# A planner that treats GpSimd and VectorE's two-port SBUF work as holders of one lock

## The chip, the cores and the metric

The kernel runs on one core of a Trainium2 chip. The metric is the device time of one execution in microseconds (us); the number used is the median of several runs. Times of single instructions are in nanoseconds (ns) or us as the profiler recorded them.

The engines are called as in the profile: PE (TensorE matmul), PEld (its weight load), DVE (VectorE), ACT (ScalarE), POOL (GpSimd) and SP (SyncE, which here issues every DMA).

## The reference

The reference is blockwise causal attention followed by two feed-forward layers, all in float32:

```python
scores = scale * np.matmul(q, k.transpose(0, 1, 3, 2))      # q, k, v: 4 x 8 x 576 x 64
scores = np.where(mask, scores, -1e9)                       # block of 64 sees itself and earlier blocks
attn = softmax(scores);  x = (attn @ v) as 2304 x 512
g = x @ w_gate;  x = (g * sigmoid(g) * (x @ w_val)) @ w_out # d_ff 1536
h = x @ w_in;  g = where(h > 0, h, exp(min(h, 0)) - 1)      # d_ff 2048
return g @ w_out
```

## The kernel before

Tokens are handled in 9 chunks of 256. Chunk 0 holds the first block of 64 tokens of every batch; chunks 1 to 8 hold the rest of a batch's tokens, two chunks for each batch. The program has three stages. The first, here called the attention stage, ends at about 470 us; it does the attention and, interleaved with it, the gate and value matmuls of the first layer (PE lines L164 to L166, tile gv). The second multiplies by the first layer's w_out (tile y). The third is the second layer, done with a seven-product scheme (tiles h and o).

Float32 matmuls are made of three products of a high part and a low part: hi x hi, hi x lo, lo x hi. The high part is a cast on ACT, the low part a subtraction. Which engine subtracts matters for this change:

- **Weights.** A conversion unit (`conv_unit`, 24 of them for gate and value, i below 2*K1) loads raw words, makes c on ACT (L142), runs three DVE steps on it (`cv_b`, L150, L152 and L154, all from SBUF to SBUF; the last two read two SBUF tensors), casts the high part wh on ACT (L157) and subtracts the low part wl on POOL (L161).
- **Heads.** For each of 64 heads, POOL makes the low parts of k (`ks`, L409), q (`ql`, L415) and v (`vs`, L422). The first 8 heads skip this. PE multiplies q by k into slo and shi in PSUM; DVE masks, takes the row maximum and scales it (nm, L481); ACT takes the exponential (L491); DVE forms 1/sum in two small steps (sm, L495 and L497). The rows are scaled on ACT for the first 20 heads and on DVE after that (`norm`, L503). PE transposes (L533, L534), ACT casts the high part th, DVE subtracts the low part tl out of PSUM (L542; tt, L568, for the last 64 keys), and PE multiplies by v (tile pv, L548 to L551 and L574). DVE adds the two halves of the result (xf, L589) and subtracts the low part xl of the chunk, from SBUF to SBUF (L596).

The order of the work on each engine is not written by hand. Class `Plan` holds a list of tasks, each with an engine, a cost in ns, a priority and its dependencies. `order` simulates them: again and again it takes the engine that can start soonest, picks among that engine's tasks that can start by then the one of least priority number, and books the engine for the task's cost. The simulated start times give the order in which the instructions are issued; each engine's instructions then run on the chip in that order, each waiting on semaphores for its inputs. In `order` before the change, engines meet only in dependencies; POOL and DVE can both be busy at the same simulated time at no extra cost. Tiles rotate over few buffers (raw 2, c 4, ks 3, ql 3, vs 4, tr 2, gv 2), and the planner also keeps the order in which such buffers are taken.

Of the kernel before, what the change touches and what calls it, by code (L numbers as in the profile page):

```python
# [13 lines left out]
ALU = mybir.AluOpType  # L14
# [27 lines left out]
class Plan:  # L42
# [9 lines left out]
        n = self.count[tag] = self.count.get(tag, -1) + 1  # L52
        return n

    def add(self, eng, ns, fn, prio, reads=(), writes=(), after=(), data=0.0, behind=None):
        i, deps, order = len(self.tasks), set(), set()
        for d in self.groups[behind] if behind else ():
            (order if self.tasks[d][0] == "SP" else deps).add(d)
        self.groups.setdefault(self.group, []).append(i)
        for k in list(reads) + list(writes):  # L60
            tag, n = b = k[:2]
            if tag in self.bufs:
                deps.update(self.users.get((tag, n - self.bufs[tag]), ()))
                order.update(self.users.get((tag, n - 1), ())[:1])
            self.users.setdefault(b, []).append(i)
        for k in list(reads) + list(after):
            if k in self.wr:
                deps.add(self.wr[k])
        for k in reads:
            self.rd.setdefault(k, []).append(i)  # L70
        for k in writes:
            if k in self.wr:
                deps.add(self.wr[k])
            deps.update(self.rd.get(k, ()))
            self.wr[k], self.rd[k] = i, []
        deps.discard(i)
        self.tasks.append((eng, ns, fn, prio, deps, data, order - deps - {i}))

    def order(self):
        T = self.tasks  # L80
        succ, left, est = [[] for _ in T], [len(t[4]) + len(t[6]) for t in T], [0.0] * len(T)
        for i, t in enumerate(T):
            for d in t[4]:
                succ[d].append((i, True))
            for d in t[6]:
                succ[d].append((i, False))
        engines = sorted({t[0] for t in T})
        ready = {e: [i for i, t in enumerate(T) if t[0] == e and not left[i]] for e in engines}
        free, dma, start = dict.fromkeys(engines, 0.0), 0.0, [0.0] * len(T)
        for _ in T:  # L90
            t, e = min((max(free[e], min(est[i] for i in ready[e])), e) for e in engines if ready[e])
            i = min((i for i in ready[e] if est[i] <= t), key=lambda i: (T[i][3], i))
            ready[e].remove(i)
            start[i] = t
            free[e] = end = t + T[i][1] * (2 if e == "PE" and t < WARM else 1)
            if T[i][5] > 0:
                dma = end = max(dma, t + DMA_IN) + T[i][5]
                end += DMA_OUT
            for j, wait in succ[i]:
                lat = 0.0 if e == "NONE" else SELF * (e == "DVE") if T[j][0] == e else LAT  # L100
                est[j] = max(est[j], end + lat + max(0.0, -T[i][5]) * (T[j][0] == "SP") if wait else t + 1.0)
                left[j] -= 1
                if not left[j]:
                    ready[T[j][0]].append(j)
        self.span = max(free.values())
        self.start = start
        return [T[i][2] for i in sorted(range(len(T)), key=lambda i: (start[i], i))]
# [3 lines left out]
def attention_moe_moe_kernel(ctx: ExitStack, tc: tile.TileContext,  # L111
# [116 lines left out]
    def conv_unit(i, prio, after=(), whole=False):  # L228
        r, c, w = ("raw", i, 0), ("c", i, 0), ("w", i, 0)
        add("SP", 450, lambda: cv_dma(i), prio, writes=[r], data=1456)  # L230
        add("ACT", 520, lambda: cv_a(i), prio, [r], [c])
        for p, ns in enumerate((335, 602, 602) if i < 2 * K1 else (500, 700, 750)):
            add("DVE", ns, lambda p=p: cv_b(i, p), prio, [r, c], [c], data=-1000 if p == 2 and i >= 2 * K1 else 0.0)
        if whole:
            return
        add("ACT", 520, lambda: cv_hi(i), prio, [c], [w], after)
        add("POOL", 1330 if i < 2 * K1 else 1500, lambda: cv_lo(i), prio, [c, w], [w])
# [45 lines left out]
    def t0_attn(s, q):  # L283
# [65 lines left out]
        add("DVE", 335, ssum, PT0, [P], [sm])  # L349
        add("DVE", 70, lambda: rec(0), PT0, [sm], [sm])  # L350
        add("DVE", 90, lambda: rec(1), PT0, [sm], [sm])
        add("DVE", 335, lambda: dve.tensor_tensor(st["P"], st["P"], st["sm"].to_broadcast([128, 4, 64]), ALU.mult), PT0, [P, sm], [P])
        add("PE", 218, tr, PT0, [P, ("id", 0, 0)], [tr_k])
        add("ACT", 264, cp, PT0, [tr_k], [pt])
        add("PE", 850, pv, PT0, [pt] + blk("vz"), [pv_k])
# [35 lines left out]
    def a_head(n, prio):  # L391
# [118 lines left out]
            add("DVE", 69, lambda u=u: sc_nm(u), prio, [nk], [nk])  # L510
            add("ACT", .833 * e + 240, lambda u=u: ex(u), prio, [sk, nk], [pk[u], sk2])
        sk2 = [("sm", n, 0), ("sm", n, 1)]
        add("DVE", 70, lambda: rec(0), prio, sk2, sk2)
        add("DVE", 81, lambda: rec(1), prio, sk2, sk2)
        for u, e in ((0, e0), (1, e1)):
            if n < NACT:
                add("ACT", .833 * e + 145, lambda u=u: norm(u), prio, [pk[u]] + sk2, [pk[u]])
            else:
                add("DVE", .521 * e + 129, lambda u=u: norm(u), prio, [pk[u]] + sk2, [pk[u]])

        ch, k = 1 + n // H, h // 2
        xr = slice(64 * j, 64 * j + 64)
# [87 lines left out]
        add("DVE", 335, xf, prio, [pvk, K["xb"]], [("xf", i, j)])  # L610
        if j == 1:
            add("ACT", 307, xh, prio, [("xf", i, 0), ("xf", i, 1)], [("x", ch, ("h", k))])
            add("POOL" if XLP else "DVE", 790 if XLP else 335, xl, prio, [("xf", i, 0), ("xf", i, 1), ("x", ch, ("h", k))], [("x", ch, ("l", k))])


    a_stage = {}
# [495 lines left out]
```

## Time and profile before

| what | value |
|---|---|
| median of 3 runs | 1046.24 us (1044.62 to 1046.64) |
| span of the profiled execution, first to last instruction | 1045.0 us |
| PE busy over the span | 1023.0 us (98%) |
| DVE, ACT, POOL busy over the span | 825.7, 606.3, 286.5 us |
| granted TensorE clock, mean | 0.998 |

The device time of the profiled execution itself is not listed beside its span; the runs lie from 0.4 us below the span to 1.6 us above it. A busy share of 98% for PE does not say that PE is at its peak, since a matmul is recorded as busy until its modelled end, and the next one may already be running: PE's pace is read from its count of matmuls and its waits, stretch by stretch.

### The profile page before, as it was taken

How to read it: one execution, taken by the hardware profiler on the slowest of the kernel's cores; microseconds unless marked ns; L12 is line 12 of the kernel's file. 1: busy time of each engine (PE TensorE's matmuls, PEld its weight loads, DVE VectorE, ACT ScalarE, POOL GpSimd, SP SyncE). 2: the span in 40 equal slices, each digit the busy share in tenths (PEclk: the TensorE clock that was granted, in tenths of full speed). 3: DMA queues.
4: the chain of work that ended last, by engine and by line, in shares of the span. 5: the costliest groups of instructions: out<-in, count | busy, mean ns of one | idle time of the engine just before them, and what ended most of it. 6: DMA issues, size and time to landing. Idle time of an engine off the chain costs nothing.

```text
span 1045.0 us, 19569 instructions
## 1 busy us (share of the span) xinstructions
PE 1023.0 (98%) x6520; PEld 935.1 (89%) x6520; DVE 825.7 (79%) x1967; ACT 606.3 (58%) x1531; POOL 286.5 (27%) x288
## 2 busy tenths in 40 slices
PE   9999899999999999999999999999999999999998
PEld 8678899999999999999977888898888998898897
DVE  6889999988888888877666775889998666876665
ACT  3898787776776677654354555555563443543343
POOL 1267543443444344303233222223210000000000
PEclk9999999999999999999999999999999999999999
DMA  7577557422542254004779988777646433454331
GB/s 177 163 217 207 154 160 202 122 80 87 139 123 81 85 140 122 25 28 134 227 258 321 316 292 282 252 237 235 218 149 211 126 121 121 122 172 121 112 111 61
DMA packets 119366, 170.00 MB, mean 163 GB/s; under 512 B 15840, under 2 KB 75744, under 8 KB 119264
## 3 DMA queue, kind: packets, MB, share of 16 engines
q1 hardware_dynamic: 119264, 168.74, 53.3%
q8 instruction: 52, 0.85, 0.3%
q14 instruction: 50, 0.41, 0.1%
HBM read 130.42 MB, written 38.27 MB: 161 GB/s over the span
## 4 chain that ended last, share of the span: by engine, by line
PE 79%; DVE 11%; DMA 4%; ACT 2%; issue 2%; SPq 1%; POOL 0%; ACTq 0%; DVEq 0%; POOLq 0%
PE gv L164 8%; PE gv L166 7%; PE gv L165 7%; PE o L893 6%; PE o L892 6%; PE o L891 6%; PE h L165 5%; PE h L166 5%; PE h L164 5%; PE y L165 3%; PE y L164 3%; PE y L166 3%; PE tr L534 2%; PE tr L533 2%; PE pv L551 2%
## 5 line engine op out<-in xcount | busy, mean ns | idle before, releaser
L164 PE MATMUL gv<-xh,wh 128*128 128x256 f32 x864 | 255.8, 296 | 0.2
L165 PE MATMUL gv<-xl,wh 128*128 128x256 f32 x864 | 241.7, 280 | 0.1
L166 PE MATMUL gv<-xh,wl 128*128 128x256 f32 x864 | 241.4, 279 | 0.0
L164 PEld LDWEIGHTS gv<-xh,wh 128*128 128x128 f32 x864 | 163.6, 189 | 4.8 <-issue 3.4
L165 PEld LDWEIGHTS gv<-xl,wh 128*128 128x128 f32 x864 | 163.8, 190 | 0.5 <-DVE xl L604 0.3
L166 PEld LDWEIGHTS gv<-xh,wl 128*128 128x128 f32 x864 | 163.3, 189 | 0.2 <-POOL wl L161 0.2
L853 DVE TENSOR_TENSOR ys<-h,ys 128x384 f32<-128x384 f32 x162 | 88.1, 554 | 69.1 <-PE h L166 66.3
L844 ACT ACTIVATE ar<-ys 128x384 f32<-128x384 f32 x96 | 50.4, 525 | 113.0 <-DVE ys L853 94.9
L165 PE MATMUL h<-yo,ws 128*128 128x384 f32 x326 | 110.1, 338 | 0.6 <-DVE yo L757 0.6
L164 PE MATMUL h<-yo,ws 128*128 128x384 f32 x326 | 109.3, 335 | 0.6 <-ACT ys L864 0.6
L166 PE MATMUL h<-yo,ws 128*128 128x384 f32 x326 | 109.6, 336 | 0.0
L409 POOL TENSOR_TENSOR ks<-rk,ks 64x576 fp32r<-64x576 f32 (+1 forms) x56 | 70.6, 1261 | 90.6 <-ACT ks L406 49.5
L165 PE MATMUL y<-al,woh 128*128 128x512 f32 (+1 forms) x240 | 89.0, 371 | 1.3 <-DVE al L669 1.1
L164 PE MATMUL y<-ah,woh 128*128 128x512 f32 (+1 forms) x240 | 88.5, 369 | 0.2 <-ACT ys L708 0.2
L166 PE MATMUL y<-ah,wol 128*128 128x512 f32 (+1 forms) x240 | 88.4, 368 | 0.0
L803 POOL TENSOR_TENSOR wm<-c,wm 128x256 fp32r<-128x256 f32 x56 | 50.6, 910 | 130.9 <-ACT wm L800 122.9
L538 ACT CAST th<-tr 128x256 fp32r<-128x256 f32 x176 | 61.3, 375 | 24.2 <-PE tr L534 22.8
L542 DVE TENSOR_TENSOR tl<-tr,th 128x256 fp32r<-128x256 f32 x176 | 69.0, 415 | 7.2 <-ACT th L538 6.5
L422 POOL TENSOR_TENSOR vs<-rv,vs 128x320 fp32r<-128x320 f32 (+1 forms) x56 | 47.2, 844 | 96.6 <-ACT vs L418 81.6
L892 PE MATMUL o<-ol,gh 128*128 128x512 f32 x180 | 71.2, 395 | 1.4 <-POOL ol L161 1.4
L893 PE MATMUL o<-oh,gl 128*128 128x512 f32 x180 | 71.5, 397 | 0.8 <-DVE gl L850 0.8
L891 PE MATMUL o<-oh,gh 128*128 128x512 f32 x180 | 70.2, 390 | 0.2 <-ACT oh L157 0.2
(149 smaller groups left out, 2673.5 us busy)
## 6 DMA issues: line engine op xcount, KB each, us to landing
ws<-w_scr SPq DMA_DIRECT2D x168, 256.0 KB, 2.7
w_scr<-wm SPq DMA_DIRECT2D x56, 256.0 KB, 3.9
a_scr<-as SPq DMA_DIRECT2D x54, 256.0 KB, 2.3
ar<-a_scr SPq DMA_DIRECT2D x108, 128.0 KB, 3.7
rk<-in_kt_dram SPq DMA_DIRECT2D x32, 288.0 KB, 4.4
raw<-in_w2i_dram SPq DMA_DIRECT2D x16, 512.0 KB, 4.7
raw<-in_w2o_dram SPq DMA_DIRECT2D x16, 512.0 KB, 4.3
rq<-in_qt_dram SPq DMA_DIRECT2D x60, 128.0 KB, 3.9
```

Of the source, the lines that this page charges most:

```text
L164: pe.matmul(dst, wh, xh, start=start, stop=False)
L165: pe.matmul(dst, wh, xl, start=False, stop=False)
L166: pe.matmul(dst, wl, xh, start=False, stop=stop)
L409: pool.tensor_tensor(st["ks"][64:128, 0:ext], raws[i][0][64:128, j, 0:ext], st["ks"][64:128, 0:ext].bitcast(F32), ALU.subtract)
L538: act.copy(st["th", c], st["tr", c][:, 0:QW])
L542: dve.tensor_tensor(st["tl", c], st["tr", c][:, 0:QW], st["th", c].bitcast(F32), ALU.subtract)
L803: add("POOL", 1000, lambda: pool.tensor_tensor(wm[n][:, 1], part(*x), wm[n][:, 0].bitcast(F32), ALU.subtract), prio, [ck(*x), hk] + whole, ...
L844: add("ACT", 500, lambda: act.activation(t(), src(), ACTF.Tanh, scale=0.5), PMP, [sk], [tk], first)
L853: add("DVE", 560, lambda: dve.tensor_tensor(hc(d), hb[b][:, 0:HT], hc(x), ALU.add), PMP, [hbk(b), hck(x)], [hck(d)])
L891: pe.matmul(d, h, OH[f], start=(p == 0 and u < 2), stop=False)
L892: pe.matmul(d, h, OL[f], start=False, stop=False)
L893: pe.matmul(d, l, OH[f], start=False, stop=(p == HP - 1 and u > 1))
```

## The change

`add` gets a flag `both`, and each task an eighth field: for any POOL task the name "DVE", for a DVE task with `both` the name "POOL", otherwise nothing. `order` keeps `port`, the simulated end of the last holder on either engine. A POOL task can't start before the last flagged DVE task has ended, and a flagged DVE task can't start before the last POOL task has ended. While a flagged task is held back, its engine may take another ready task that isn't. When two engines could start at the same time, the one that was not the last holder goes first.

Flagged on DVE are: the three steps of the 24 gate and value conversion units, the scaling of the first chunk's probabilities (L352), the first small step of 1/sum (L495), the row scaling on DVE (L503) and xl (L596). No instruction is added, removed or altered, and no cost is changed. The conversion units of the later weights run the same three DVE steps and aren't flagged; POOL's tasks are holders in every stage. Nothing on the chip enforces the order between the two engines: the change is in the order of each engine's own queue.

```diff
-    def add(self, eng, ns, fn, prio, reads=(), writes=(), after=(), data=0.0, behind=None):
+    def add(self, eng, ns, fn, prio, reads=(), writes=(), after=(), data=0.0, behind=None, both=False):
...
-        self.tasks.append((eng, ns, fn, prio, deps, data, order - deps - {i}))
+        self.tasks.append((eng, ns, fn, prio, deps, data, order - deps - {i}, {"POOL": "DVE", "DVE": both and "POOL"}.get(eng)))
...
+        port, last = {"POOL": 0.0, "DVE": 0.0}, None
+
+        def at(i):
+            return max(est[i], port[T[i][7]]) if T[i][7] else est[i]
+
         for _ in T:
-            t, e = min((max(free[e], min(est[i] for i in ready[e])), e) for e in engines if ready[e])
-            i = min((i for i in ready[e] if est[i] <= t), key=lambda i: (T[i][3], i))
+            t, _, e = min((max(free[e], min(at(i) for i in ready[e])), e == last, e) for e in engines if ready[e])
+            i = min((i for i in ready[e] if at(i) <= t), key=lambda i: (T[i][3], i))
             ready[e].remove(i)
             start[i] = t
             free[e] = end = t + T[i][1] * (2 if e == "PE" and t < WARM else 1)
+            if T[i][7]:
+                port[e], last = end, e
...
-            add("DVE", ns, lambda p=p: cv_b(i, p), prio, [r, c], [c], data=-1000 if p == 2 and i >= 2 * K1 else 0.0)
+            add("DVE", ns, lambda p=p: cv_b(i, p), prio, [r, c], [c], data=-1000 if p == 2 and i >= 2 * K1 else 0.0, both=i < 2 * K1)
...
-        add("DVE", 335, lambda: dve.tensor_tensor(st["P"], st["P"], st["sm"].to_broadcast([128, 4, 64]), ALU.mult), PT0, [P, sm], [P])
+        add("DVE", 335, lambda: dve.tensor_tensor(st["P"], st["P"], st["sm"].to_broadcast([128, 4, 64]), ALU.mult), PT0, [P, sm], [P], both=True)
...
-        add("DVE", 70, lambda: rec(0), prio, sk2, sk2)
+        add("DVE", 70, lambda: rec(0), prio, sk2, sk2, both=True)
...
-                add("DVE", .521 * e + 129, lambda u=u: norm(u), prio, [pk[u]] + sk2, [pk[u]])
+                add("DVE", .521 * e + 129, lambda u=u: norm(u), prio, [pk[u]] + sk2, [pk[u]], both=True)
...
-            add("POOL" if XLP else "DVE", 790 if XLP else 335, xl, prio, [("xf", i, 0), ("xf", i, 1), ("x", ch, ("h", k))], [("x", ch, ("l", k))])
+            add("POOL" if XLP else "DVE", 790 if XLP else 335, xl, prio, [("xf", i, 0), ("xf", i, 1), ("x", ch, ("h", k))], [("x", ch, ("l", k))], both=True)
```

## Rows read from the trace of the kernel before

**Rows 1.** The page: span, and busy time of each engine.

```profile
span 1045.0 us, 19569 instructions
...
PE 1023.0 (98%) x6520; PEld 935.1 (89%) x6520; DVE 825.7 (79%) x1967; ACT 606.3 (58%) x1531; POOL 286.5 (27%) x288
```

**Rows 2.** Stretches: length, then engines' busy us (instructions), PEclk, DMA share, GB/s.

```profile
52.00:78.00 26.00, 24.63 (x161) 19.11 (x160) 22.15 (x54) 23.69 (x66) 17.91 (x15) 1.00 0.80 218
78.00:104.00 26.00, 23.68 (x184) 22.15 (x183) 25.53 (x58) 21.66 (x54) 19.86 (x17) 1.00 0.76 209
104.00:130.00 26.00, 23.52 (x178) 22.58 (x177) 24.92 (x55) 19.55 (x49) 13.88 (x12) 0.93 0.50 154
...
26.00:130.00 104.00, 97.11 (x652) 80.33 (x651) 94.22 (x235) 85.99 (x227) 57.88 (x46) 0.98 0.66 186
...
156.00:468.00 312.00, 308.94 (x2593) 305.25 (x2592) 270.95 (x870) 216.86 (x658) 120.96 (x131) 1.00 0.37 104
```

**Rows 3.** DVE groups by shape, 26 to 130 us: count | busy us, mean ns | idle.

```profile
L154 DVE SCALAR_TENSOR_TENSOR c<-raw,c 128x512 int32<-128x512 int32 x20 | 20.6, 1028 | 0.0
L152 DVE SCALAR_TENSOR_TENSOR c<-raw,c 128x512 int32<-128x512 int32 x20 | 19.0, 950 | 0.2
L150 DVE TENSOR_SCALAR c<-c 128x512 int32<-128x512 int32 x20 | 10.6, 530 | 0.9 <-ACT c L142 0.7
...
L495 DVE TENSOR_SCALAR sm<-sm 128x2 f32<-128x2 f32 x13 | 3.4, 263 | 0.5 <-ACT ph L491 0.3
```

**Rows 4.** Single DVE lines, 26 to 130 us: duration ns min/median/max, starts.

```profile
L150 DVE TENSOR_SCALAR c<-c x20: 405/420/1303, 26.6 to 126.2; 128x512 int32<-128x512 int32 x20
...
L152 DVE SCALAR_TENSOR_TENSOR c<-raw,c x20: 673/744/1664, 27.2 to 126.9; 128x512 int32<-128x512 int32 x20
...
L154 DVE SCALAR_TENSOR_TENSOR c<-raw,c x20: 666/752/1866, 28.2 to 128.8; 128x512 int32<-128x512 int32 x20
...
L495 DVE TENSOR_SCALAR sm<-sm x13: 156/169/1224, 33.3 to 122.5; 128x2 f32<-128x2 f32 x13
...
L596 DVE TENSOR_TENSOR xl<-xf,xh x2: 419/926/1432, 97.4 to 125.6; 128x256 fp32r<-128x256 f32 x2
...
L497 DVE RECIPROCAL sm<-sm x13: 143/165/168, 33.5 to 122.7; 128x2 f32<-128x2 f32 x13
```

**Rows 5.** Timeline near 97 us: start us, duration us, instruction [idle before <-releaser].

```profile
97.08 1.44 POOL L409 TENSOR_TENSOR ks<-rk,ks 64x576 fp32r<-64x576 f32 x1 [0.85 <-POOL vs L422]
...
97.36 1.43 DVE L596 TENSOR_TENSOR xl<-xf,xh 128x256 fp32r<-128x256 f32 x1
...
99.52 0.19 PEld L551 LDWEIGHTS pv<-tl,vs 128*128 128x128 f32 x1 [0.79 <-DVE tl L542]
```

**Rows 6.** Timeline from 106 to 109 us.

```profile
106.18 1.42 POOL L161 TENSOR_TENSOR wl<-c,wh 128x512 fp32r<-128x512 f32 x1
106.39 1.22 DVE L495 TENSOR_SCALAR sm<-sm 128x2 f32<-128x2 f32 x1
...
108.48 0.47 PE L440 MATMUL slo<-ks,qh 128*128 128x448 f32 x1 [2.09 <-ACT pl L491]
```

**Rows 7.** Waits of PEld, 26 to 130 us: total us, times, longest us.

```profile
PEld pv L551 <- DVE tl L542: 3.6, 7, 1.0
...
PEld slo L440 <- ACT pl L491: 2.3, 1, 2.3
PEld pv L548 <- DVE xl L604: 2.1, 2, 1.0
...
PEld pv L574 <- DVE tt L568: 1.1, 2, 0.7
```

**Rows 8.** DVE group by shape, 52 to 104 us.

```profile
L154 DVE SCALAR_TENSOR_TENSOR c<-raw,c 128x512 int32<-128x512 int32 x9 | 11.1, 1237 | 0.0
```

**Rows 9.** Timeline: the 24th low weight part on POOL, and its first matmul.

```profile
139.55 1.29 POOL L161 TENSOR_TENSOR wl<-c,wh 128x512 fp32r<-128x512 f32 x1 [2.73 <-ACT wh L157]
...
141.37 0.28 PE L166 MATMUL gv<-xh,wl 128*128 128x256 f32 x1
```

## The prediction

> **What bounds the kernel now.** I read the page first [rows 1]: PE is busy 98% of the span, so only what keeps PE from its next matmul can move the time. The table of stretches comes next [rows 2]. From 156 to 468 us PE is busy 308.94 of 312 us with 2593 matmuls, 8.3 in a us; from 26 to 130 us it issues 652 in 104 us, 6.3 in a us, and is idle for 104 - 97.11 = 6.9 us. Part of that lower pace is dearer work (the first heads multiply in plain float32), so the pace alone doesn't price a loss; the waits do. In the same stretch DVE is busy 94.22 of 104 us, and from 78 to 130 us (25.53 + 24.92) / 52 = 97%: there DVE is the fullest engine, and what lengthens its queue reaches PE.
>
> Then I read DVE's instructions by shape and by line [rows 3, 4]. The same instruction on the same shape takes 666 ns at best and 1866 at worst (L154), 673 and 1664 (L152), 405 and 1303 (L150), 156 and 1224 (L495, two elements a row). L497, as small but not flagged, stays within 143 to 168. So some DVE instructions are held up inside their own time, and the timeline says by whom: xl starts at 97.36 us, takes 1.43 us instead of 0.42, and ends at 98.79; POOL's ks ran from 97.08 to 98.52 [rows 5]. The step L495 starts at 106.39 and ends at 107.61, just where POOL's wl from 106.18 ends, 107.60 [rows 6].
>
> The price to DVE from 26 to 130 us is count times (mean minus least): L154 20 x (1028 - 666) = 7.2 us, L152 20 x (950 - 673) = 5.5, L150 20 x (530 - 405) = 2.5, L495 13 x (263 - 156) = 1.4, L596 2 x (926 - 419) = 1.0. Together 17.7 us of the 94.22 are waiting.
>
> Last, what of it reaches PE. After the held xl the subtraction tl is late and the weight load for pv idles 0.79 us [rows 5]; after the held L495 the row maximum, the exponential and with them the next slo are late, and PE idles 2.09 us [rows 6]. The weight loads' waits of this sort, on tl, on the slo buffer, on xl of the first heads and on tt, are 3.6 + 2.3 + 2.1 + 1.1 = 9.1 us [rows 7]. The granted clock of 104 to 130 us is 0.93, the only one of these stretches under 1 [rows 2]; PE had idled for 2.09 us inside that stretch. A part of it at the lower of the two levels, 1.2 instead of 2.4 GHz, costs 26 x (1 - 0.93) = 1.8 us.
>
> **The change part by part.** It adds and removes no instruction, so no direct cost enters: the whole effect is another order on each queue, and SP's loads follow the orders that free their buffers.
>
> *Flagged DVE steps move.* The planner now sees that a flagged step can't run beside POOL, and fills DVE with unflagged ready work (tl, gv's epilogue, row maxima) while POOL holds the lock. On the chip the wait inside the flagged step becomes useful time if the two queues keep step with the plan. The plan's costs fit what the rows show when nobody is in the way: its 335, 602 and 602 ns for the three conversion steps stand against 405, 673 and 666 as recorded (neighbours overlap a little), and 1460 for a ks of 576 against 1.44 us [rows 4, 5]. What it left out was the lock. Ends: nothing is gained if the engines drift so far that holders meet by chance as before; all 17.7 us of DVE's waits go if none meets. I take half, 8.8 us of DVE's time: POOL and DVE are coupled through ACT's casts, so they keep step partly, but nothing on the chip holds POOL back when DVE comes late.
>
> *What PE gets.* Between nothing and all of the 9.1 us and the 1.8 us of clock, 10.9 us. Half of the waits and half of the clock is 4.6 + 0.9 = 5.5 us. The reason for a half is the one above: the waits follow DVE's held steps.
>
> *Later, 156 to 468 us.* PE's idle time is 312 - 308.94 = 3.1 us in all [rows 2]; ends 0 and 3.1, and I count nothing, since tl and tt wait there behind ordinary work as well.
>
> *POOL's tasks move back.* They now wait in the plan for flagged DVE steps of up to 0.67 us. Their cover is POOL's idle time, 104 - 57.88 = 46 us between 26 and 130 us, mostly waits for ACT's casts. No wait for a POOL result is among the large waits of PEld [rows 7]. Nothing, then; without that cover, ks or wl late by one step is 0.67 us each time.
>
> *After the attention stage* there are no flagged DVE tasks, so POOL's `port` bound is an old time and the plan keeps its shape, shifted. The later weights' steps meet POOL as before. Nothing.
>
> *Sum.* 1045.0 - 5.5 = 1039.5 us of span. The runs' median is 1.2 us above the profiled span: 1040.7, said as 1041 us.
>
> By the Trainium skill (SBUF — State Buffer, section on SBUF's two separate sides), DVE and GpSimd share a port pair that is locked for a whole instruction, by a DVE operation with two SBUF inputs or in a two-port mode, and the loser blocks fully. The trace agrees: L495 was held to 107.61 us by a POOL operation that ended at 107.60. The rule also says that no order makes the two sides' work run side by side, which makes a rival of it, the second below.
>
> **The rivals.** *First: the conversion starves (slower).* A held DVE step can only start when POOL has ended and DVE is free at that moment. DVE nearly always has other ready work, which it now takes first and which runs past POOL's end; POOL, if it has a task ready, takes the lock again. Each of a unit's three steps can lose a turn, one POOL operation of 1.3 to 1.4 us, so a unit is 3 x 1.3 to 1.4 = 3.9 to 4.3 us later. Gate and value tiles are taken in a fixed order, so PE can't jump over a late weight. The 24th low part is ready at 139.55 + 1.29 = 140.84 us and its first matmul starts at 141.37, a slack of 0.53 us [rows 9]: the rival decides once DVE's gain up to there is less than the delay less 0.5 us. If the last units each come one turn late without any gain, four of them cost 4 x 1.3 = 5.2 us, and 1046.2 + 5.2 = 1051 us. For it: PE's pace hangs on these units, with two raw buffers only. Against it: while non-flagged work lasts, PE's waits on tl and tt shrink, and once PE waits for weights that work dries up and DVE comes free for the flagged steps.
>
> *Second: the lock itself is full.* From 52 to 104 us POOL's operations take 17.91 + 19.86 = 37.77 us [rows 2] and nine conversion units [rows 8] at 405 + 673 + 666 = 1744 ns take 15.7 us: 53.5 us in 52, with some of POOL's own waiting in it. No order makes room there, so the waits only change sides: DVE's go, and weights and ks come later by as much. What is left is 104 to 130 us, where POOL needs just 13.88 us [rows 2]: the 2.3 us wait for slo and the 1.8 us of clock, of which half is 2 us. That gives 1044 to 1046 us. For it: the sum. Against it: most weights of that stretch have no matmul waiting for them in the rows, so they can be late at no cost.
>
> *Third: all of it goes.* 10.9 us and the 3.1 us of the later stretch, 14 us in all: 1032 us. Against it: queues that drift.
>
> *Fourth: no change that shows.* Engines out of step meet by chance as before: 1046 us.
>
> **How the numbers follow.** Forecast (2 to 9 us faster) 0.45; everything goes (over 9 us) 0.12; lock full or no change, 0.16 in all; starved conversion or any other lateness that outweighs the gain 0.27. A difference of 0.2%, 2.1 us, is about what a measurement of this kernel can tell from none. So faster is 0.45 + 0.12 = 0.57, same 0.16, slower 0.27. The range runs from 1034, just above the end where everything goes, to 1051, the end of the first rival: about 0.07 lies below and 0.10 above. The forecast's own range is 1037 to 1044 us.
>
> **What would show it.** Right: from 26 to 130 us the mean of L152 and L154 falls from 950 and 1028 ns toward 670 and DVE is busy less than 94.22 us for the same work; PEld's waits on tl, slo and tt fall to half of 9.1 us; the clock of 104 to 130 us is 1.00; and the stage ends some 5 us sooner. The 24th low weight part then ends before 140.84 us. Wrong: DVE's means fall, but PE or PEld waits for wl or wh, the first rival; POOL's durations or idle time grow as DVE's fall and the weights come later, the second; the means stay, the fourth. I would also be wrong if a new order on PE itself, a gap of some us at a chunk's end, took back what DVE gave; no row of before can show that.

## The result, and the profile after

The changed kernel takes 1057.42 us (median of 4 runs, 1053.56 to 1062.15) against 1046.44 us for the kernel before: a ratio of 1.0104, with a 95% interval of 1.0065 to 1.0144. It is slower by 11 us, beyond the top of my range. The profiled execution has a span of 1051.8 us and took 1053.56 us. In the changed kernel the lines above L100 are 7 higher: L150, L152 and L154 are L157, L159 and L161, wh is L164, wl is L168, and the gate and value matmuls are L171 to L173.

The first stage isn't over when its attention is, at 470 us: the last gate and value matmul starts at 509.0 us before the change. Where this text says how far the first stage got, it goes by the start of that matmul, and by the start of the 24th and last low weight part wl on POOL, 139.6 us before the change.

The page, as in [rows 1]:

```profile
span 1051.8 us, 19578 instructions
...
PE 1022.9 (97%) x6520; PEld 936.1 (89%) x6520; DVE 808.4 (77%) x1967; ACT 606.8 (58%) x1531; POOL 284.3 (27%) x288
```

The stretches, with the columns of [rows 2]; the first line is the one stretch of the kernel before that [rows 2] doesn't show, the others are of the changed kernel:

```profile
130.00:156.00 26.00, 25.35 (x208) 24.77 (x209) 23.94 (x73) 21.33 (x61) 12.70 (x14) 1.00 0.52 156
...
52.00:78.00 26.00, 24.52 (x172) 20.26 (x171) 18.86 (x53) 23.71 (x67) 17.47 (x18) 1.00 0.83 220
78.00:104.00 26.00, 21.85 (x152) 20.59 (x152) 21.58 (x53) 17.73 (x42) 12.58 (x10) 0.87 0.49 153
104.00:130.00 26.00, 22.53 (x180) 21.36 (x178) 21.53 (x53) 15.90 (x40) 15.45 (x14) 1.00 0.60 177
...
26.00:130.00 104.00, 94.90 (x639) 79.14 (x637) 81.88 (x227) 79.54 (x212) 54.70 (x46) 0.97 0.65 184
130.00:156.00 26.00, 22.08 (x150) 19.67 (x150) 22.36 (x58) 22.51 (x59) 11.43 (x11) 0.93 0.49 140
156.00:468.00 312.00, 311.01 (x2630) 309.90 (x2631) 264.13 (x880) 219.36 (x666) 119.66 (x133) 1.00 0.38 105
```

From 78 to 104 us PE issues 152 matmuls where it issued 184 before, at a granted clock of 0.87, and from 130 to 156 us 150 where it issued 208, at 0.93. From 156 to 468 us it is the other way round: PE's idle time falls from 3.1 to 1.0 us. DVE, the fullest engine before, is now busy 81.88 of 104 us where it was busy 94.22 [rows 2]: it isn't full any more, and PE is slower all the same. The DVE groups, 26 to 130 us, with the columns of [rows 3]:

```profile
L159 DVE SCALAR_TENSOR_TENSOR c<-raw,c 128x512 int32<-128x512 int32 x18 | 14.6, 809 | 0.4 <-DVE slo L481 0.3
L161 DVE SCALAR_TENSOR_TENSOR c<-raw,c 128x512 int32<-128x512 int32 x18 | 14.1, 783 | 0.1
L157 DVE TENSOR_SCALAR c<-c 128x512 int32<-128x512 int32 x17 | 9.3, 545 | 0.4 <-ACT c L149 0.4
L502 DVE TENSOR_SCALAR sm<-sm 128x2 f32<-128x2 f32 x13 | 3.5, 284 | 1.7 <-ACT ph L498 1.7
```

Two of the single lines in the same stretch, with the columns of [rows 4]:

```profile
L159 DVE SCALAR_TENSOR_TENSOR c<-raw,c x18: 677/692/1625, 25.4 to 125.5; 128x512 int32<-128x512 int32 x18
...
L161 DVE SCALAR_TENSOR_TENSOR c<-raw,c x18: 672/683/1623, 26.4 to 127.1; 128x512 int32<-128x512 int32 x18
```

Counted as in the prediction, with the least times of [rows 4] for L157 and L502, DVE's waits are 18 x (809 - 677) + 18 x (783 - 672) + 17 x (545 - 405) + 13 x (284 - 156) = 8.4 us. They were 17.7. About half of the waits went, then, as forecast; the time went elsewhere. It was the two-source steps that gained: L152 and L154 together waited 12.7 us and now wait 4.4, while the one-source steps, L150 and L495, waited 3.9 us and now wait 4.0. The weight loads' waits of the same stretch, with the largest on top, say where:

```profile
PEld gv L171 <- ACT wh L164: 4.6, 3, 2.5
PEld gv L173 <- POOL wl L168: 3.3, 3, 1.2
...
PEld gv L171 <- ACT xh L608: 1.4, 1, 1.4
...
PEld slo L447 <- ACT pl L498: 0.6, 1, 0.6
...
PEld pv L558 <- DVE tl L549: 0.5, 1, 0.5
```

The waits on tl and on the slo buffer, 3.6 and 2.3 us before [rows 7], are almost gone. In their place stand waits on the weights, wh and wl, which in the kernel before come to 0.2 us each in the whole run. Why the weights are late is read from the timeline. These are the three DVE steps of the 11th conversion unit in the kernel before (start us, duration us, instruction):

```profile
68.77 0.41 DVE L150 TENSOR_SCALAR c<-c 128x512 int32<-128x512 int32 x1
...
69.98 0.69 DVE L152 SCALAR_TENSOR_TENSOR c<-raw,c 128x512 int32<-128x512 int32 x1
...
70.71 1.25 DVE L154 SCALAR_TENSOR_TENSOR c<-raw,c 128x512 int32<-128x512 int32 x1
```

The same unit in the changed kernel:

```profile
69.89 0.84 DVE L157 TENSOR_SCALAR c<-c 128x512 int32<-128x512 int32 x1
...
76.51 0.68 DVE L159 SCALAR_TENSOR_TENSOR c<-raw,c 128x512 int32<-128x512 int32 x1
...
79.78 0.67 DVE L161 SCALAR_TENSOR_TENSOR c<-raw,c 128x512 int32<-128x512 int32 x1
```

And some of POOL's operations between the first of these steps and the second:

```profile
72.21 0.88 POOL L429 TENSOR_TENSOR vs<-rv,vs 128x320 fp32r<-128x320 f32 x1 [0.19 <-ACT vs L425]
73.05 0.75 POOL L422 TENSOR_TENSOR ql<-rq,qh 128x256 fp32r<-128x256 f32 x1
74.21 0.88 POOL L429 TENSOR_TENSOR vs<-rv,vs 128x320 fp32r<-128x320 f32 x1 [0.41 <-ACT vs L425]
75.17 1.45 POOL L416 TENSOR_TENSOR ks<-rk,ks 64x576 fp32r<-64x576 f32 x1
```

Before, the unit takes 3.2 us on DVE with a wait in it (68.77 to 71.96). After, its steps hardly wait and take 10.6 us (69.89 to 80.45): between them stand the k, q and v parts of several heads on POOL, in the plan holders of the lock one after the other, and on DVE the other work that was let past. This is the worst of the 24 units; from the start of the first step to the end of the third a unit takes 3.9 us on DVE in the mean, where it took 3.2. But it is the one that loses the lead: the 10th unit ends on DVE 1.5 us sooner than before (64.9 against 66.4 us), the 11th 8.5 us later. At 87.78 us PE has stood still for the wh of the 12th; the granted clock of that stretch is 0.87:

```profile
87.78 0.47 PE L171 MATMUL gv<-xh,wh 128*128 128x256 f32 x1 [2.30 <-ACT wh L164]
89.33 0.58 PE L173 MATMUL gv<-xh,wl 128*128 128x256 f32 x1 [0.87 <-POOL wl L168]
```

The last of the 24 low parts:

```profile
150.55 1.29 POOL L168 TENSOR_TENSOR wl<-c,wh 128x512 fp32r<-128x512 f32 x1
```

It ends at 150.55 + 1.29 = 151.84 us, 11.0 us later than before [rows 9]. The last gate and value matmul and the last of the second stage are read from the line's count, durations and first and last start, before:

```profile
L166 PE MATMUL gv<-xh,wl x864: 276/279/415, 24.6 to 509.0; 128*128 128x256 f32 x173
L166 PE MATMUL y<-ah,wol x240: 283/389/402, 481.5 to 659.4; 128*128 128x512 f32 x96, 128*128 128x256 f32 x24
```

And after:

```profile
L173 PE MATMUL gv<-xh,wl x864: 276/280/580, 23.1 to 513.0; 128*128 128x256 f32 x173
L173 PE MATMUL y<-ah,wol x240: 281/389/398, 487.3 to 662.8; 128*128 128x512 f32 x96, 128*128 128x256 f32 x24
```

In this execution 3.4 us are lost by the end of the second stage. The last stage grows from 1045.0 - 659.4 = 385.6 to 1051.8 - 662.8 = 389.0 us, another 3.4. PE's waits there, 650 to 850 us (total us, times, longest us), the two largest before:

```profile
PE o L892 <- POOL ol L161: 1.4, 1, 1.4
PE o L893 <- DVE gl L850: 0.8, 1, 0.8
```

And after:

```profile
PE h L171 <- DVE ys L860: 3.3, 3, 2.1
PE h L172 <- DVE yo L764: 1.2, 1, 1.2
```

No flagged DVE step runs there, and yet its order is a new one.

These are 6.8 us of span, in the fastest of the changed kernel's four executions. What else the median holds can be estimated from the granted clock, which goes down as the time goes up: 0.991, 0.988, 0.986 and 0.980 for 1053.56, 1057.03, 1057.82 and 1062.15 us. The span times what the clock lacks to 1 is an estimate, from above, of what the lower clock cost, since it costs nothing while PE waits. At the median it is 13.7 us here; in the runs of the kernel before that went with the experiments it is 3 to 6 us (median clocks of 0.997 to 0.994). At like clocks the two kernels are near each other: two executions of the kernel before that went with `pool_writes_long` took 1050.36 us at 0.990 and 1056.28 us at 0.985. So by this estimate most of the 11 us was spent at the lower clock. In the profiled execution, 78 to 104 and 130 to 156 us are under 1, and in both PE is idle for some 4 us. Its first 26 us are at 0.87 too, but so they are in `pool_writes` below, the fastest kernel of all. For the executions without a trace, what lowered the clock isn't shown.

### The profile page after: what moved, and what is told of

It reads as the page before. It is cut to its first block, busy times and chain, and to the rows that moved or that the text cites. A ratio compares the mean times of both kernels' runs of the same rounds, so it can differ in the third digit from the quotient of the medians.

```text
span 1051.8 us, 19578 instructions
## 1 busy us (share of the span) xinstructions
PE 1022.9 (97%) x6520; PEld 936.1 (89%) x6520; DVE 808.4 (77%) x1967; ACT 606.8 (58%) x1531; POOL 284.3 (27%) x288
## 4 chain that ended last, share of the span: by engine, by line
PE 85%; DVE 6%; DMA 3%; ACT 3%; issue 2%; SPq 1%; POOL 0%; ACTq 0%; DVEq 0%
PE gv L171 9%; PE gv L173 9%; PE gv L172 9%; PE o L899 6%; PE o L900 6%; PE o L898 6%; PE h L172 5%; PE h L173 5%; PE h L171 5%; PE y L172 3%; PE y L173 3%; PE y L171 3%; PE tr L541 2%; PE tr L540 2%; PE pv L558 2%; PE pv L557 2%
## 5 line engine op out<-in xcount | busy, mean ns | idle before, releaser
L171 PE MATMUL gv<-xh,wh 128*128 128x256 f32 x864 | 256.0, 296 | 6.1 <-ACT wh L164 4.1
L173 PE MATMUL gv<-xh,wl 128*128 128x256 f32 x864 | 242.6, 281 | 2.6 <-POOL wl L168 2.6
L171 PEld LDWEIGHTS gv<-xh,wh 128*128 128x128 f32 x864 | 164.1, 190 | 11.4 <-ACT wh L164 4.6
L173 PEld LDWEIGHTS gv<-xh,wl 128*128 128x128 f32 x864 | 164.0, 190 | 3.5 <-POOL wl L168 3.5
L171 PE MATMUL h<-yo,ws 128*128 128x384 f32 x326 | 109.7, 336 | 4.2 <-DVE ys L860 3.3
L173 PE MATMUL h<-yo,ws 128*128 128x384 f32 x326 | 109.7, 336 | 0.0
L416 POOL TENSOR_TENSOR ks<-rk,ks 64x576 fp32r<-64x576 f32 (+1 forms) x56 | 68.2, 1218 | 87.1 <-ACT ks L413 49.9
L171 PE MATMUL y<-ah,woh 128*128 128x512 f32 (+1 forms) x240 | 88.3, 368 | 0.0
L173 PE MATMUL y<-ah,wol 128*128 128x512 f32 (+1 forms) x240 | 88.3, 368 | 0.0
L549 DVE TENSOR_TENSOR tl<-tr,th 128x256 fp32r<-128x256 f32 x176 | 69.2, 415 | 10.6 <-ACT th L545 9.9
L429 POOL TENSOR_TENSOR vs<-rv,vs 128x320 fp32r<-128x320 f32 (+1 forms) x56 | 44.1, 789 | 101.8 <-ACT vs L425 75.8
L171 PEld LDWEIGHTS h<-yo,ws 128*128 128x128 f32 x326 | 61.2, 188 | 11.4 <-DVE ys L860 4.2
```

The costliest lines, as they stand in the source:

```text
L171: pe.matmul(dst, wh, xh, start=start, stop=False)
L173: pe.matmul(dst, wl, xh, start=False, stop=stop)
L416: pool.tensor_tensor(st["ks"][64:128, 0:ext], raws[i][0][64:128, j, 0:ext], st["ks"][64:128, 0:ext].bitcast(F32), ALU.subtract)
L549: dve.tensor_tensor(st["tl", c], st["tr", c][:, 0:QW], st["th", c].bitcast(F32), ALU.subtract)
```

## The experiments

Three theories. **One:** the conversion steps are pushed back, and late weights stop PE. **Two:** any new plan of this greedy planner lands some us off. **Three:** holding POOL's k, q and v parts back is what costs. Ratios below are to the kernel before, timed on the same chip, with their 95% intervals.

### Which flags

`conv_only`: all `both=True` are taken back, `both=i < 2 * K1` stays. `no_conv`: the reverse.

> Only the three DVE steps of the 24 gate and value conversion units are flagged. Theory one, the conversion steps starve behind POOL: as slow as the full change, 1052 to 1062 us, with PE waiting for wh and wl between 80 and 150 us and the granted clock under 1 there. Theory two, any new plan of this greedy planner lands some us off, whatever is flagged: anything from 1040 to 1060 us, with no waits for wh and wl in particular. Theory three, holding POOL's k, q and v parts back is what costs: some of the loss, 1048 to 1054 us, with PE waiting on slo for ks and ql.

Measured: 1.0090 (1.0055 to 1.0125). The 24th wl starts at 165.0 us, and the last gate and value matmul at 521.1. The time is what theory one expected, but not the waits: for wl PE waits 0.8 us in all, for wh none that shows, though the weights are later than in any other run. Its longest waits, 20 to 480 us, the three largest:

```profile
PE pv L558 <- DVE tl L549: 3.0, 6, 1.5
PE gv L171 <- DVE as L652: 2.6, 2, 1.3
PE pv L557 <- DVE xf L596: 2.1, 3, 1.0
```

> The 24 conversion units are not flagged; the scaling of the first chunk, the first step of 1/sum, the row scaling on DVE and xl still are. Theory one, starving conversions: near the kernel before, 1043 to 1049 us, and no wait of PE for wh or wl. Theory two, any new plan: anything from 1040 to 1060 us. Theory three, POOL held back: these flagged steps hold POOL back too, though more briefly, 1047 to 1052 us.

Measured: 1.0028 (1.0006 to 1.0050). The 24th wl starts at 137.8 us, the last gate and value matmul at 506.7, 2.3 us sooner than before; the last stage is longer. So the loss before the last stage hangs on the conversion's flags, as theory one has it, but late weights are not always what PE waits for. The median of no_conv, 1050.10 us, lies in the range of theory three and above that of theory one; conv_only, 1056.72 us, lies above theory three's.

### A new plan for no reason

```diff
-LAT, SELF, DMA_IN, DMA_OUT = 300.0, 100.0, 1300.0, 900.0
+LAT, SELF, DMA_IN, DMA_OUT = 301.0, 100.0, 1300.0, 900.0
```

> The kernel before, with no flags, and the planner's latency between engines set to 301 instead of 300 ns: a new plan for no reason. Theories one and three: within 2 or 3 us of the kernel before. Theory two: off by 5 us and more.

Measured: 1.0026 (1.0006 to 1.0046), 2.7 us. So a new plan for no reason costs a quarter of the loss, in the one case tried, and no_conv can't be told from it. All the runs together say more. Seven orders book DVE's conversion steps behind POOL (the change, conv_only, dve_waits, in_place, fair_lock, conv_early, first_by_change): they lose 0.89 to 1.38%. Six don't (no_conv, lat_301, pool_waits, late_weights, later_by_change, no_conv_first): they lose 0.26 to 0.62%. No new plan was faster than the old one.

### One side of the lock at a time

In `dve_waits` only DVE's flagged steps are held back in the plan, in `pool_waits` only POOL's tasks.

```diff
-            return max(est[i], port[T[i][7]]) if T[i][7] else est[i]
+            return max(est[i], port[T[i][7]]) if T[i][7] == "POOL" else est[i]   # dve_waits
+            return max(est[i], port[T[i][7]]) if T[i][7] == "DVE" else est[i]    # pool_waits
```

> Only one side of the lock: a flagged DVE step waits for POOL in the plan, POOL waits for nobody. Theory one: at least as slow as the change, 1055 us and more, with the 24th low weight part at 150 us or later. Theory of POOL held back: the loss is gone, 1043 to 1050 us.

> Only the other side: POOL waits in the plan for flagged DVE steps, no DVE step is passed over or delayed. Theory one: the weights come as before, the 24th low part near 141 us, 1043 to 1050 us. Theory of POOL held back: as slow as the change, 1052 us and more, PE waiting for ks, ql or wl.

Measured: dve_waits 1.0089 (1.0053 to 1.0125), with the 24th wl at 145.9 us, sooner than the 150 us that theory one expected, and the last gate and value matmul at 513.0, as with the change. pool_waits 1.0049 (1.0026 to 1.0073), with the 24th wl at 139.6 us and the last gate and value matmul at 508.7, as before (139.6 and 509.0). Theory three falls as the main cause: holding POOL back alone costs under half of the loss. What pool_waits loses is not in its weights. Its profile, one of its faster executions with a span of 1046.1 us, shows 1.9 us in the last stage (1046.1 - 658.6 = 387.5 us); where its median loses the rest, this doesn't show. Both orders keep the change's new rule for ties, which no run takes out by itself; together with POOL's waits in the plan it costs the 0.49% of pool_waits.

### Three ways to keep the lock and spare the conversion

`in_place`: DVE takes its task as before the change and books the wait.

```diff
-            return max(est[i], port[T[i][7]]) if T[i][7] else est[i]
+            return max(est[i], port["DVE"]) if T[i][0] == "POOL" else est[i]
...
             ready[e].remove(i)
+            if e == "DVE" and T[i][7]:
+                t = max(t, port["POOL"])
```

> All flags as in the change, but a flagged DVE step isn't passed over: the planner picks DVE's task as before the change, books the wait for POOL on DVE, and lets POOL wait for that step to end. The plan knows the lock and starves nobody. Theory one: the loss is gone, 1038 to 1047 us, with no wait for wh or wl above 1 us. Theory two: anything from 1040 to 1060 us. Theory three: POOL is held back more than in the change, so as slow or slower, 1055 us and more.

Measured: 1.0138 (1.0104 to 1.0171), the slowest of all. Theory one in its first form, that being passed over is the cause, falls here: nobody is passed over, and the 24th wl still starts at 149.1 us. `fair_lock` lets POOL give way (a part of the edit):

```diff
...
+                    if e == "POOL":
+                        p = min(T[i][3] for i in ready[e] if at(i) <= t)
+                        if any(T[j][7] and est[j] <= t and T[j][3] < p for j in ready["DVE"]):
+                            continue
+                        t = max(t, now)
...
```

> The change, and POOL in the plan gives way to a flagged DVE step that is ready and has the smaller priority number. Theory one, conversion steps lose their turns to POOL: the 24th low weight part is back near 141 us (151.8 us with the change), the attention stage ends near 509 us, and the whole takes 1042 to 1050 us. Theory of bad luck in planning: no tie to the weights, 1045 to 1060 us. Theory of POOL held back: slower than the change, 1058 us and more. The run in_place was against theory one in its first form (nobody passed over, yet 1062 us); if this one is slow too, with late weights, passing over is not the cause but the lock itself as the plan books it.

Measured: 1.0111 (1.0074 to 1.0148), with the 24th wl at 149.4 us. `conv_early` is the change with CLEAD 44.0 in place of 24.0:

> The change, with the conversion units' priority moved 20 us ahead (CLEAD 44 instead of 24). If late weights are a matter of priority, the loss shrinks to 1045 to 1050 us. If they come from lost turns at the lock (theory one), priority can't help a step that is passed over while POOL holds, and it stays at 1052 us or more.

Measured: 1.0124 (1.0082 to 1.0166). My expectation was wrong in its means: priority did bring the weights (the 24th wl starts at 142.0 us), and it did not help. What stands in the way now is another queue. PE's longest wait in fair_lock, 26 to 160 us:

```profile
PE pv L569 <- DVE tl L560: 7.1, 4, 3.8
```

And in conv_early:

```profile
PE tr L540 <- ACT pl L508: 13.2, 1, 13.2
```

So weights that come in time are not enough: where the plan books the lock on the conversion's steps, the weights come late (by 6 to 25 us) or, in conv_early, the heads do.

### The lock taken away on the chip

`pool_writes` leaves the order of before as it is and takes away what makes holders meet, POOL's reading:

```diff
-        pool.tensor_tensor(lo, cv_state.pop(i)[1], hi.bitcast(F32), ALU.subtract)
+        c_of = cv_state.pop(i)[1]
+        if i < 2 * K1:
+            for _ in range(2):
+                pool.memset(lo.bitcast(F32), 0.0)
+        else:
+            pool.tensor_tensor(lo, c_of, hi.bitcast(F32), ALU.subtract)
...
```

The subtractions for ks, ql and vs are replaced in the same way.

> The kernel before in its own order, but POOL makes no low parts in the attention stage: each subtraction is two memsets of zero to the same tile, so that POOL reads nothing and the low parts of gate and value weights, k, q and v are zero. This takes the lock away without a new order. If waits at the lock cost what I said of the attention stage, DVE's waits of 17.7 us between 26 and 130 us fall under 3 us, PE's waits on tl, slo and tt by more than half, and the time falls by 5 to 11 us, to 1035 to 1041 us. If DVE's waits were hidden anyway, it stays at 1044 us or more though they are gone. If DVE is held up by a writing POOL too, its waits stay.

Measured: 1029.16 us, 0.9844 (0.9820 to 0.9869), 16.3 us faster. The stretch from 26 to 130 us:

```profile
26.00:130.00 104.00, 102.54 (x738) 87.86 (x737) 88.41 (x262) 93.60 (x246) 43.06 (x98) 1.00 0.75 211
```

The three conversion steps in it, durations as least, median and most:

```profile
L150 DVE TENSOR_SCALAR c<-c x21: 406/421/809, 27.8 to 123.8; 128x512 int32<-128x512 int32 x21
...
L152 DVE SCALAR_TENSOR_TENSOR c<-raw,c x21: 671/683/747, 28.3 to 124.6; 128x512 int32<-128x512 int32 x21
...
L154 DVE SCALAR_TENSOR_TENSOR c<-raw,c x22: 665/682/693, 26.2 to 125.3; 128x512 int32<-128x512 int32 x22
```

PE issues 738 matmuls in the stretch where it issued 652 [rows 2], and its clock is 1.00 throughout. Counted as in the prediction, DVE's waits fall from 17.7 to 2.7 us, under the 3 us expected: most of the lock is gone, and most of what is left is on the one-source steps, 21 x (465 - 406) ns for L150 and 14 x (208 - 154) ns for the first step of 1/sum. The gain is more than the 5 to 11 us expected, and more than the 10.9 us that I had put as the upper end. POOL is also busy for less time here, and its steps no longer wait for ACT's casts (wl for wh), so three memsets were tried in place of two:

> As pool_writes with three memsets in place of two, so that POOL is busy longer than with its subtractions (near 65 us instead of 57.9 between 26 and 130 us). If the missing lock made pool_writes fast, 1028 to 1033 us here too; if POOL's shorter time did, 1040 us and more.

Measured: 0.9866 (0.9827 to 0.9906), with POOL busy 65.80 us of the 104, more than the 57.88 of before. A shorter POOL is not the reason. That the low parts come earlier, and free the buffers that they read from earlier, could not be split off in this way. Before, the weight loads waited for wl 0.2 us in the whole run and for ks 0.3, so earlier low parts had little to give by themselves; what the buffers give isn't shown.

Now the same under the change's order, and two others:

> The changed kernel in its own order, with POOL's subtractions of the attention stage replaced by two memsets of zero each, as in pool_writes (low parts of gate and value weights, k, q and v are zero). If the change's order itself costs, this stays 8 us or more above pool_writes: 1037 to 1045 us. If the loss of the change came from waits at the lock in new places, the two are alike, 1027 to 1032 us.

> The order of no_conv (all flags but those of the conversion units), with POOL's subtractions of the attention stage replaced by two memsets of zero each. If the place of the conversion steps is what makes the change's order bad, this is near pool_writes, 1029 to 1035 us (3 to 5 us of it from the last stage's new order). If the other flagged steps do harm as well, 1040 us and more.

> The order of in_place, with the same memsets. If its order is bad by itself, 1048 us and more, as change_pool_writes; if it was the lock on the chip, under 1040 us.

| order of | POOL reads | POOL only writes | the lock's share |
|---|---|---|---|
| before | 1 | 0.9844 (0.9820 to 0.9869) | 1.56%, 16 us |
| no_conv | 1.0028 (1.0006 to 1.0050) | 0.9875 (0.9814 to 0.9936) | 1.53%, 16 us |
| the change | 1.0104 (1.0065 to 1.0144) | 1.0064 (1.0032 to 1.0097) | 0.40%, 4 us |
| in_place | 1.0138 (1.0104 to 1.0171) | 1.0080 (1.0050 to 1.0111) | 0.58%, 6 us |

With POOL only writing, the change's order takes 1052.12 us, even more than the 1037 to 1045 us that I expected if the order costs; the orders of in_place, 1057.43 us, and of no_conv, 1034.86 us, came out in the ranges given for them. The shares are differences of the two ratios, uncertain by 0.25% in the first row and 0.5 to 0.65% in the others, and they hold whatever POOL's reading brings with it, the earlier low parts too. This settles the main point. The change's order, with most of the lock gone, is 2.20% slower than the order of before with most of it gone, 23 us, uncertain by 4; by the clock estimate some 7 of them are lower clock (10.5 against 3.1 us at the median). The 11th conversion unit shows the order at work: it still ends on DVE at 79.2 us, where it ends at 68.2 in pool_writes. The lock's share under the change's order is 4 us, not clear of nothing, where it was 16. Twelve saved and 23 paid make the 11 that was measured; that sum comes out by the way the table is made and proves nothing more. Nor does the change avoid all of the twelve: DVE's waits fell only by half, to 8.4 us (3.0 with POOL only writing), and what is left of them costs little where PE waits for other things. no_conv saves nothing that is clear of the noise and pays 0.3% with the lock, about what lat_301 pays. In change_pool_writes the stretch from 26 to 130 us reads:

```profile
26.00:130.00 104.00, 93.92 (x644) 78.43 (x642) 76.97 (x229) 80.87 (x217) 38.27 (x86) 0.98 0.67 188
```

L159, the second conversion step, is held up nowhere in it:

```profile
L159 DVE SCALAR_TENSOR_TENSOR c<-raw,c x19: 674/691/694, 25.8 to 129.8; 128x512 int32<-128x512 int32 x19
```

And the weight loads wait for wh all the same:

```profile
PEld gv L176 <- ACT wh L164: 4.7, 3, 2.3
PEld tr L550 <- ACT ph L517: 4.3, 2, 3.8
```

DVE is busy 77 of 104 us and PE issues 644 matmuls, with idle time on every engine: PE idles 10 of the 104 us, POOL 66. No engine is full; the queues wait for each other in the order that they were given.

### Later weights without a lock

> The kernel before without flags, with the conversion units' priority 8 us later (CLEAD 16 instead of 24). If late weights are enough to make the loss, the 24th low part comes near 150 us instead of 140.8, PE waits for wh and wl, and the time is 1050 to 1058 us. If they aren't, it stays within 4 us of before.

Measured: 1.0035 (1.0006 to 1.0064). CLEAD 16 made the 24th wl only 3.6 us later (143.2 us), and PE waits for tl (4.7 us), not for weights. As a test of whether late weights are enough it is inconclusive.

### The stages' orders, put together

`first_by_change` plans the whole without the lock first, chains the later stages' tasks on each engine in that order, and plans again with the lock. `later_by_change` is the reverse, and `no_conv_first` does the first with no_conv's flags.

```diff
...
+        self.run(False)                     # True for later_by_change
+        chain = []
+        for e in ("ACT", "DVE", "PE", "POOL", "SP"):
+            q = sorted((i for i in late if self.tasks[i][0] == e), key=lambda i: (self.start[i], i))
+            chain += zip(q, q[1:])
+        return self.run(True, chain)        # False for later_by_change
...
```

> The attention stage is planned with the lock, but the tasks of the two later stages keep on every engine the order that they had among themselves before the change. If the loss is all of the attention stage, 1052 to 1058 us as with the change. If the 3.3 us that the last stage lost came from its own new order, 1048 to 1052 us, with the last stage (after the last y matmul) back from 388.9 to about 386 us.

> The reverse: the attention stage is planned without the lock, and the later stages' tasks keep among themselves the order that the change gave them. If their new order costs by itself, the last stage takes 388 to 390 us and the whole 1048 to 1051 us; if not, 1045 to 1048 us. The attention stage should end at 509 us as before.

> The flags without the conversion units (as in no_conv), and the later stages in the order of the kernel before. The attention stage of no_conv ended 2.3 us sooner than before and its last stage took 4.6 us longer; if the two parts add, this gives 1042 to 1045 us, the best so far. If the orders of the stages can't be put together like that, 1047 to 1051 us.

Measured: first_by_change 1.0110 (1.0084 to 1.0136), later_by_change 1.0033 (1.0017 to 1.0050), no_conv_first 1.0062 (1.0036 to 1.0089). The last stage takes 1056.7 - 669.5 = 387.2 us in the first and 1046.8 - 656.7 = 390.1 in the second, whose PE waits there are those of the change to the digit:

```profile
PE h L183 <- DVE ys L872: 3.3, 3, 2.1
PE h L184 <- DVE yo L776: 1.2, 1, 1.2
```

So the later stages' new order alone costs 0.33%, 3.5 us. The first stage's order alone costs as much as the whole change, within the intervals; the parts don't add up exactly. no_conv_first was to be the best version and isn't: its last gate and value matmul starts at 509.7 us, not at 506.7.

### One small holder out

```diff
             if op == 0:
-                dve.tensor_scalar(st["sm"], st["sm"], EPS, None, ALU.add)
-            else:
+            if op == 1:
                 dve.reciprocal(st["sm"], st["sm"])
```

> The kernel before in its own order, without the step that adds 1e-9 to the row sums (L495). A sum holds the exponential of the row's maximum less itself, which is 1, and 1e-9 more changes no float32 of 1 and above. It takes away 64 small holders of the lock: 1.4 us of DVE's waits between 26 and 130 us, 64 x 0.15 us of DVE time, and near 106 us the wait that PE paid with 2.1 us and some clock. Expected 1041 to 1045 us against 1045 to 1046; if those were hidden, no change within 0.2%.

Measured: 0.9991 (0.9960 to 1.0021). No change that shows, but the interval holds both what I expected and nothing at all. In its trace PE's wait for slo between 100 and 116 us is 0.6 us where it was 2.1, and the granted clock from 104 to 130 us is 1.00 where it was 0.93; why the time doesn't show it stays open. None of the versions that compute the whole beats the kernel before.

## Why the prediction was wrong

- **What bounds the kernel: right, and larger than said.** DVE's waits at the lock reach PE; with POOL only writing, the order of before is 16.3 us faster, not at most 10.9, nor the 14 of the third rival. The upper end counted the weight loads' waits on four tiles; the 86 matmuls more from 26 to 130 us show that PE's slower pace held more. How much of the 16.3 us is earlier low parts and not the lock isn't shown.
- **Flagged DVE steps move: right in size, in part by luck.** I took half of 17.7 us; 9.3 us went and 8.4 are left. The means of L152 and L154 fell toward 670 ns as said. But the half is made of two-source steps that lost two thirds of their waits and one-source steps that lost none, which I didn't foresee.
- **What PE gets: this step failed.** It let PE gain half of its waits because DVE lost half of its own, 5.5 us, and gave the new order itself no price ("so no direct cost enters"). PE gained nothing: from 26 to 130 us its idle time went from 6.9 to 104 - 94.90 = 9.1 us. The order had the largest price of all, 23 us with POOL only writing. DVE's saved waits turned into idle time, 104 - 94.22 = 9.8 us before and 104 - 81.88 = 22.1 after. The clock was a gain of 0.9 us in the sum; by the estimate above it is most of the loss.
- **The first rival: right in place, short in price.** It named the conversion steps, the lost turns, the fixed order of the gate and value tiles and the 24th low part. It expected four turns of 1.3 us, 5.2 in all; the 24th low part came 11.0 us late. Its chance of 0.27 rested on the thought that DVE would come free for the flagged steps; by 78 us DVE was free, and its queue's order kept it from using that: it idles 0.72 us before 78.26 us, while the 11th unit's third step, whose input was done at 77.19, stands further back in its queue. As the only cause, being passed over is too narrow: in_place passes nobody over and loses too, and in conv_only the weights are later still and PE hardly waits for them.
- **The second rival: partly right.** The waits changed sides, weights for tl, as it said of a full lock. But with most of the lock away the change's order loses all the same, so a full lock isn't what stops PE.
- **Later, 156 to 468 us: I counted nothing, and it gained.** PE's idle time there fell from 3.1 to 1.0 us, of the 3.1 that I had put as the upper end. That the flags did it isn't shown: in lat_301, without any, it fell to 1.4.
- **POOL's tasks move back: right for the weights, not shown for the time.** pool_waits alone leaves the weights and the last gate and value matmul where they were, but costs 0.49%, 5 us, where I had put nothing.
- **After the attention stage: wrong.** I put a shifted but equal plan there, at nothing. The planner gives the last stage another order, and that costs 3.5 us. Whether it does so for the other start or for the new rule for ties wasn't tried.
- **Open:** in conv_only, in_place, fair_lock and conv_early PE waits in different places. That such an order is bad by itself is shown for the change and in_place (1.0064 and 1.0080 with POOL only writing); that one cause lies behind them all isn't shown.

## What to carry to other kernels

A truer cost in a greedy planner needn't make a better plan: it changes what the greedy rule picks next, and that has a price of its own, which a profile of the kernel before can't show. Price an edit of an order by what comes later through it, not only by the wait that it removes, and measure the two apart, by running old and new order with the contended resource taken away. And look at the stages that the edit isn't about: here their new order cost 3.5 us by itself, though with the change's first stage the old one brought nothing (first_by_change).

## What the runs showed of the hardware

A step of two elements a row can hold DVE as long as a large one: L495 took up to 1224 ns beside a reading POOL and at best 156 [rows 4]. With POOL only writing, the two-source steps L152 and L154 stay at 747 and 693 ns at most, while the one-source L150 still reaches 809 against 406, from 120.25 to 121.06 us, beside memsets of wl: so this one-source step from SBUF to SBUF is held even by a POOL that reads nothing. By the Trainium skill (SBUF — State Buffer, section on SBUF's two separate sides) an operation with two SBUF inputs meets only a GpSimd operation that reads SBUF, and one in a two-port mode meets any. The runs agree with the first half; they agree with the second if L150 runs in such a mode, which no run shows.

The changed kernel's runs spread from 1053.56 to 1062.15 us with mean granted clocks from 0.991 to 0.980. In the profiled one the stretch with PE's wait of 2.30 us has a clock of 0.87, between its two levels, 1.2 and 2.4 GHz: near 85 us, before the wait, a gate and value matmul takes 0.28 us, and near 91 us, after it, 0.41. By the estimate used above that costs up to 26 x 0.13 = 3.4 us, so this gap of PE cost more than its length.
